# Attention and two gated layers on one core: Strassen's scheme for a whole block in the first layer's second pass, and an order amended by a table

## The chip, the core and the metric

The kernel runs on one core of a Trainium2 chip. The metric is the time of one execution in device microseconds, from the first to the last instruction of the program with what lies around it; smaller is better. Each kernel is run several times and the median is given.

## The reference, cut to what matters

Attention within chunks of 64 positions, then two layers that every token passes. All arrays are float32; there are 4608 tokens (8 x 576) of 512 features.

```
out = softmax(q_chunk @ k_chunk.T / 8) @ v_chunk        # 8 heads of 64, chunks of 64
x   = out as 4608 tokens x 512
g   = x @ w_gate            # 512 x 1536
val = x @ w_val             # 512 x 1536
x   = (silu(g) * val) @ w_out        # 1536 x 512     first layer
h   = x @ w_in              # 512 x 2048
out = (h * sigmoid(1.702 h)) @ w_out2   # 2048 x 512  second layer
```

Because single products of the fast format are too coarse, every float32 operand is split in a high part and a rest ("hi" and "lo"), and each product is made of three: hi by hi, hi by lo, lo by hi (helper `mm3`, lines 406 to 408).

## The kernel before

**Tiles and passes.** The tokens are cut in nine blocks of 512 (`NB`, `BT`). The hidden features of each layer are cut in halves, so there are four passes over the nine blocks: passes 0 and 1 for the first layer, 2 and 3 for the second. Pass 0 also makes the attention of the next blocks and turns weights into hi and lo on the way (`conv_tile`, `conv_part`, lines 476 to 484); pass 0's sums of a block go to DRAM (`y_dram`) and pass 1 loads them and adds its own. In pass 1 the weights of layer 2 are converted.

**First product.** In a pass of layer 1 a block has three groups (`group_products`), each of four hidden tiles of 128 (two of the gate, two of the value). A group's product is made by Strassen's scheme: seven products (`product`) of 12 matmuls of 256 columns in place of eight, written to two banks of PSUM, and put together by ScalarE copies (tile `u`) and VectorE additions (tile `c`, line 399).

**Second product.** `gated` takes silu of the gate on ScalarE, multiplies on VectorE (tile `h`), and splits into `hh` and `hl`. `second` then multiplies with a weight tile `o` (three matmuls of 512 columns into one of four banks, `ys`): per block 6 hidden tiles by 4 output tiles, 24 such steps, without Strassen. `block_sum` adds the four banks to what pass 0 left (`yv`, then `xr`), and `x_to_dram` makes from a finished block the seven combinations of its token quarters (`token_combos`), hi and lo, and stores them for layer 2 (`x_dram`). In layer 2 both products use Strassen's scheme (`group_gated`, `last_product`), and the blocks' inputs are loaded again (`x_load`).

**What sets the order.** Every step is recorded as an operation with an engine, an estimate of its length and a priority (`Program.op`). `order` plans the five queues (TensorE "PE", VectorE "DVE", ScalarE "ACT", GpSimd "POOL", and one DMA queue on SP) from these; `dues` works back from the end; `emit` repeats this 28 times with amended keys, judges each order by `replay` and keeps the best. The instructions are then issued engine by engine in that order, and each engine takes its own strictly in turn. Buffers come from rings: `o` has three tiles of 512 KB, `x` eight, `xr` one.

## Time and profile before

| | |
|---|---|
| median of three runs | 1688.71 us (1688.47 to 1689.58) |
| the profiled execution | 1689.54 us |
| its span, first to last instruction | 1687.2 us |
| TensorE busy | 1658.1 us, 98% |
| VectorE, ScalarE, GpSimd busy | 65%, 53%, 43% |
| share of the chain that ended last that lies on TensorE | 84% |
| mean busy share of the 16 DMA engines, per 1/40 of the span | between 0.3 and 0.9 or more, mostly 0.7 to 0.9 |

How to read it: the numbers of a row are microseconds from the start of the span, unless marked ns. TensorE's matmuls are pipelined, so a row's duration is longer than the step from one matmul's start to the next; the step is read from two starts. Idle time stands with the engine that was waited for. The passes can be told by their DMAs: the last store of pass 0's sums is issued at 543 us, the first load of them in pass 1 at 547 us, and the first weight tile of layer 2's second product at 961 us.

### The profile page before, as it was taken

What the parts mean: (1) busy time and instruction counts of PE and PEld (TensorE: products, weight loads), DVE (VectorE), ACT (ScalarE), POOL (GpSimd) and SP (SyncE); (2) the same over time, 40 slices, a digit from 0 to 9 for tenths busy, and PEclk for the clock granted to TensorE, in tenths of its full rate; (3) what the DMA queues carried; (4) which work ended last, traced back from release to release, by engine and by line L of the source; (5) the groups of instructions that cost most, each with busy time, mean ns of one, the idle gap of its engine ahead of it and who ended that gap; (6) DMA issues with size and microseconds to landing.
All of it is one profiled execution on the core that took longest, in us unless ns stands there. A gap on an engine that the chain in (4) does not pass through costs nothing.

```text
span 1687.2 us, 36353 instructions
## 1 busy us (share of the span) xinstructions
PE 1658.1 (98%) x14428; PEld 1579.5 (94%) x14428; DVE 1098.8 (65%) x1606; ACT 892.2 (53%) x1511; POOL 726.0 (43%) x736
## 2 busy tenths in 40 slices
PE   7989999999999999999999999999999999999998
PEld 7878999889999999999999999999999999999998
DVE  6878877787764566644544477787755556555556
ACT  6876677777644444433333456555544444444443
POOL 2675516564444555541211235676731133333333
PEclk8999999999999999999999999999999999999999
DMA  7567788887899899887679998999989977777773
GB/s 293 177 237 276 271 273 301 284 288 258 281 333 342 305 330 325 304 283 243 233 247 337 375 334 299 312 318 317 311 262 339 348 231 232 233 238 236 235 257 109
DMA packets 184153, 472.65 MB, mean 280 GB/s; under 512 B 19760, under 2 KB 44848, under 8 KB 183728
## 3 DMA queue, kind: packets, MB, share of 16 engines
q1 hardware_dynamic: 183984, 470.34, 81.7%
q8 instruction: 114, 1.87, 0.4%
q14 instruction: 55, 0.45, 0.1%
HBM read 331.84 MB, written 138.41 MB: 279 GB/s over the span
## 4 chain that ended last, share of the span: by engine, by line
PE 84%; DVE 4%; DMA 3%; ACT 3%; issue 2%; POOL 2%; SPq 0%; POOLq 0%; DVEq 0%; ACTq 0%
PE banks L406 28%; PE banks L408 27%; PE banks L407 27%; PE banks L667 1%; DMA od_b<-ws 1%; DVE c L399 1%; PE banks L662 1%; DMA raw<-in_moe_w_out 1%; DVE xt L399 1%; DVE t L481 1%; PE banks L732 1%; ACT L718 0%; POOL ws L399 0%; DMA raw<-in_moe_w_in 0%; POOL wc L399 0%
## 5 line engine op out<-in xcount | busy, mean ns | idle before, releaser
L399 DVE TENSOR_TENSOR c<-u,banks 128x512 f32<-128x512 f32 x312 | 213.2, 683 | 307.4 <-PE banks L408 192.2
L406 PE MATMUL banks<-x,wc 128*128 128x256 f32 x1044 | 297.5, 285 | 3.2 <-ACT u L390 2.9
L407 PE MATMUL banks<-x,wc 128*128 128x256 f32 x1044 | 294.6, 282 | 0.0
L408 PE MATMUL banks<-x,wc 128*128 128x256 f32 x1044 | 294.5, 282 | 0.0
L390 ACT COPY u<-banks 128x512 f32<-128x512 f32 x261 | 152.9, 586 | 248.4 <-PE banks L408 247.2
L406 PE MATMUL banks<-x,wb 128*128 128x256 f32 x744 | 213.3, 287 | 4.2 <-ACT x L390 2.4
L406 PE MATMUL banks<-x,wa 128*128 128x256 f32 x744 | 211.3, 284 | 2.1 <-DVE c L399 1.6
L407 PE MATMUL banks<-x,wb 128*128 128x256 f32 x744 | 211.5, 284 | 0.8 <-DVE x L399 0.8
L408 PE MATMUL banks<-x,wb 128*128 128x256 f32 x744 | 211.4, 284 | 0.0
L407 PE MATMUL banks<-x,wa 128*128 128x256 f32 x744 | 210.0, 282 | 1.1 <-POOL x L399 1.1
L406 PEld LDWEIGHTS banks<-x,wc 128*128 128x128 f32 x1044 | 198.3, 190 | 13.2 <-ACT u L390 6.0
L408 PE MATMUL banks<-x,wa 128*128 128x256 f32 x744 | 210.0, 282 | 0.0
L407 PEld LDWEIGHTS banks<-x,wc 128*128 128x128 f32 x1044 | 198.4, 190 | 6.5
L408 PEld LDWEIGHTS banks<-x,wc 128*128 128x128 f32 x1044 | 198.9, 191 | 0.0
L406 PE MATMUL banks<-hh,o 128*128 128x512 f32 x432 | 173.5, 402 | 0.3 <-ACT hh L390 0.3
L408 PE MATMUL banks<-hh,o 128*128 128x512 f32 x432 | 172.6, 400 | 0.0
L407 PE MATMUL banks<-hl,o 128*128 128x512 f32 x432 | 170.8, 395 | 0.2 <-DVE hl L399 0.2
L974 ACT ACTIVATE xr<-c 128x512 f32<-128x512 f32 x136 | 86.0, 632 | 153.9 <-DVE c L399 149.8
L406 PEld LDWEIGHTS banks<-x,wb 128*128 128x128 f32 x744 | 142.7, 192 | 11.2 <-ACT x L390 2.5
L407 PEld LDWEIGHTS banks<-x,wb 128*128 128x128 f32 x744 | 142.8, 192 | 5.3 <-DVE x L399 1.0
L406 PEld LDWEIGHTS banks<-x,wa 128*128 128x128 f32 x744 | 141.0, 190 | 6.8 <-DVE c L399 2.8
L407 PEld LDWEIGHTS banks<-x,wa 128*128 128x128 f32 x744 | 140.9, 189 | 4.7 <-POOL x L399 1.7
(227 smaller groups left out, 4494.6 us busy)
## 6 DMA issues: line engine op xcount, KB each, us to landing
x<-x_dram SPq DMA_DIRECT2D x182, 512.0 KB, 5.5
o<-od_b SPq DMA_DIRECT2D x119, 512.0 KB, 4.6
o<-od_a SPq DMA_DIRECT2D x102, 512.0 KB, 5.1
x_dram<-x SPq DMA_DIRECT2D x56, 512.0 KB, 5.8
wd_b<-ws SPq DMA_DIRECT2D x56, 256.0 KB, 4.7
od_b<-ws SPq DMA_DIRECT2D x56, 256.0 KB, 4.6
raw<-in_moe_w_out SPq DMA_DIRECT2D x44, 255.8 KB, 4.8
wd_a<-ws SPq DMA_DIRECT2D x42, 256.0 KB, 4.2
```

Of the source, the lines that this page charges most:

```text
L390: op("act", act_us(n), lambda: nc.scalar.copy(out=dst.ap, in_=cut(src.ap)), [src], [dst], prio, near=near)
L399: lambda: e.tensor_tensor(out=dst.ap, in0=of_a(a.ap), in1=of_b(b.ap), op=by), [a, b], [dst], prio, near=near)
L406: nc.tensor.matmul(o, ah, bh, start=first, stop=False, **kind)
L407: nc.tensor.matmul(o, ah, bl, start=False, stop=False, **kind)
L408: nc.tensor.matmul(o, al, bh, start=False, stop=last, **kind)
L481: op("dve", dve_us(n), lambda: nc.vector.scalar_tensor_tensor(out=t.ap.bitcast(I32), in0=t.ap, scalar=-4096 * up, in1=word(1).bitcast(F32) ...
L662: nc.tensor.matmul(un.s.ap[h64(b), a, h64(g)], un.q.ap[h64(a), cs], un.k.ap[h64(a), cs], start=True, stop=True)
L667: nc.tensor.matmul(un.o.ap[h64(b), a, h64(2 * g + c)], un.v.ap[h64(a), cs], un.e.ap[h64(a), cs], start=True, stop=True)
L732: nc.tensor.transpose(pt.ap[:, cs], e.ap[:, cs], ident.ap)
L974: op("act", act_us(512), lambda: nc.scalar.activation(out=h.ap, in_=c.ap, func=AF.Gelu_apprx_sigmoid), [c], [h], prio, "gelu")
```

## The change

Five things are changed together.

1. In pass 1 the second product of a whole block is made by Strassen's scheme. The gated values of the block's six hidden tiles are kept as four quarters (256 tokens by 384 hidden features, `hidden`, `gated_quarters`); `hidden_part` makes seven combinations and their hi and lo (768 elements per partition each); `second_part` multiplies each with its weight combination in three steps of six matmuls of 256 columns, 21 steps in place of 24, into three banks. The result is added to pass 0's sums, which are loaded straight into `xr`. The weight combinations are made in pass 0 (`y_combos`, `out_pair`) and stored in `yw_dram`; a load of `o` brings two of the 21.
2. `x_to_dram` writes the lo over its own source (`xt`, `xr`) and the hi into the area that holds the hidden parts. Only the last block but one is made into `x` tiles, which stay in SBUF and are what layer 2 begins with; pass 2 takes the blocks in the order 7, 0 to 6, 8 and pass 3 begins with block 8, whose tiles are still there (`BLOCKS`).
3. The rings `q`, `k`, `v`, `h`, `e`, `yv`, `hh`, `hl` become places in three areas (`Stage`: `sr`, `sf`, `sp`) that pass 1 uses in another way.
4. `replay` is gone. The planner's order is amended by a table, `PLACES`: it names operations that move to another engine or behind another operation, some hundreds for each engine.
5. Some of the planner's estimates are altered (0.72 for 0.8, 1.18 for 1.3, 6.0 for 8.0).

```
+PLACES = {
+    "pe": (
+        "4:9,44,61,22,19,21,8 5:26,10,18,24,17,27,52 7:13 11:15,6,20 78:54,69 23:28 25:16 209:244 "
...
+    def amended(self, seq):
+        queue = {eng: [o for o in seq if o.eng == eng] for eng in self.FREE}
+        runs = [(eng, *run.split(":")) for eng, places in PLACES.items() for run in places.split()]
+        for eng, _, ns in runs:
+            for n in ns.split(","):
+                o = self.ops[int(n)]
+                queue[o.eng].remove(o)
+                o.eng = eng
+        for eng, behind, ns in runs:
+            i = queue[eng].index(self.ops[int(behind)]) + 1 if int(behind) >= 0 else 0
+            queue[eng][i:i] = [self.ops[int(n)] for n in ns.split(",")]
...
+        j = passes[1][1].index(g)
+        def out_pair(prio):
+            t0, t1 = [conv_tile((g.name, "o", i), g.outs[i], prio) for i in range(2)]
+            for n, (m, src, cut) in enumerate(y_combos(t0, t1, prio)):
...
+                store(yw_dram[:, i], s, [yw_done[i]], prio + n)
...
     def x_to_dram(xb, b, prio):
...
+        if b == NB - 2:
+            X[2, b] = [None] * 7
+            for n, (m, src, cut) in enumerate(combos):
+                i = ORDER[2].index(m)
+                X[2, b][i] = x = ring["x"].new([P, 2, 2, HT], F32R)
+                split(*[x.part(lambda ap, c=c: ap[:, c]) for c in range(2)], src, 512, prio + n, ("dve", "pool")[n % 2], cut)
+                store(x_dram[1][:, b, i], Buf(lambda x=x: x.ap.rearrange("p c a t -> p (c a t)"), None, None, x), [xd[1][b][i]], prio + n + 2)
+            return
...
+                t = stage[2].take(n % 4 * 3, 2)
...
+            lo = Buf(lambda src=src, cut=cut: cut(src.ap).bitcast(F32R), None, None, src)
...
+    YORDER = "1326574"
...
+    def gated_quarters(y, j, c, prio):
+        js = slice(j * 256, (j + 1) * 256)
...
+            op("act", act_us(512), lambda ap=ap, i=i: nc.scalar.activation(
+                out=ap(), in_=c[i].ap[:, :, 0], func=AF.Silu), [c[i]], qs, prio, "silu")
+            op("dve", dve_us(512), lambda ap=ap, i=i: nc.vector.tensor_tensor(
+                out=ap(), in0=ap(), in1=c[i].ap[:, :, 1], op=ALU.mult), [*qs, c[i]], qs, prio)
...
+    def hidden_part(y, label, prio):
...
+            tt(src, b22, b11, ALU.subtract, 768, prio, T_ENG[1])
...
+        hi, lo = [stage[2].take(k % 2 * 6 + 3 * c, 3) for c in range(2)]
+        split(hi, lo, src, 768, prio, Y_LO[k])
+        if label == "1":
+            tt(b11, b12, b11, ALU.subtract, 768, prio, T_ENG[0])
+        elif label == "3":
+            tt(b12, b22, b12, ALU.subtract, 768, prio, T_ENG[2])
+        elif label == "6":
+            tt(src, src, b21, ALU.subtract, 768, prio + 2, T_ENG[3])
...
+        if k % 2 == 0:
+            n = min(2, 21 - k)
+            w4 = ring["o"].new([P, 2, 2, 256], F32R)
...
+        def fn():
+            ts = slice(j * 256, (j + 1) * 256)
+            for e in range(2):
+                es = slice(e * P, (e + 1) * P)
+                mm3(m.ap[:, e], w.ap[:, 0, es], w.ap[:, 1, es], hi.ap[:, ts], lo.ap[:, ts],
+                    e == j == 0 and not goes_on, j == 2, skip_group_check=True)
+        op("pe", OS, fn, [w, hi, lo], [m], prio)
...
+    BLOCKS = [range(NB), range(NB), [NB - 2, *range(NB - 2), NB - 1], [NB - 1, NB - 2, *range(NB - 2)]]
...
-                elif end and nxt[0] < NPASS:
-                    x_load(*nxt, start[nxt[0]][nxt[1]] - 18)
+                elif end and nxt == (3, 0):
+                    X[3, b] = xs
+                elif end and nxt[0] < NPASS and nxt != (2, 0):
+                    x_load(nxt[0], BLOCKS[nxt[0]][nxt[1]], start[nxt[0]][nxt[1]] - 18)
```

What the built programs show at three places follows. First ScalarE in the opening, where pass 0's first block is made and the exponentials of the first units stand among the silu of the first products (`h`, after the change `sr`). The kernel before:

```order
L916 ACT_TABLE_LOAD
L916 ACTIVATE h<-banks 128x256
L478 ACTIVATE wb_273<-wb_273,offset 128x512 x2
L735 COPY c<-banks 128x512
L718 ACT_TABLE_LOAD
L718 ACTIVATE e<-e 128x512
L476 ACTIVATE t<-wa_318,offset 128x512
L390 CAST x<-banks 128x4x128
L390 COPY xr<-banks 128x4x128
L916 ACT_TABLE_LOAD
```

The same place after the change:

```order
L661 ACTIVATE t<-wa_231,offset 128x512
L936 COPY c<-banks 128x512 x2
L919 ACTIVATE sf<-sf 128x512
L1136 ACT_TABLE_LOAD
L1136 ACTIVATE sr<-banks 128x256
L573 CAST x<-banks 128x4x128 x2
L573 COPY xr<-banks 128x4x128
```

The exponential of the next unit now stands ahead of the first silu, so that one load of the table stands there in place of three.

Second VectorE within a block of pass 1. Before, where `c` is a sum of the first product, `h` the gated values, `hl` their lo, `xr` the block's sum:

```order
L399 TENSOR_TENSOR c<-u,banks 128x512
L399 TENSOR_TENSOR xr<-yv,banks 128x512
L399 TENSOR_TENSOR c<-u,banks 128x512
L399 TENSOR_TENSOR h<-h,c 128x512
L399 TENSOR_TENSOR c<-u,banks 128x512
L399 TENSOR_TENSOR hl<-h,hh 128x512
```

After the change, where `sf` and `sr` hold the quarters and `sp` the lo of a combination:

```order
L581 TENSOR_TENSOR c<-u,banks 128x512 x4
L581 TENSOR_TENSOR sp<-sf,sp 128x768
L581 TENSOR_TENSOR sp<-sr,sp 128x768 x2
L581 TENSOR_TENSOR sf<-sf 128x768
L581 TENSOR_TENSOR sr<-sr,sf 128x768
L581 TENSOR_TENSOR sf<-sr,sf 128x768
L581 TENSOR_TENSOR xr<-xr,banks 128x2x256 x2
L581 TENSOR_TENSOR sp<-sr,sp 128x768
L581 TENSOR_TENSOR sp<-sf,sp 128x768
L581 TENSOR_TENSOR sr<-sr 128x768
```

Seven lo and four combinations of 768 elements and nine additions into `xr` per block stand in the place of six lo of 512 and four additions.

Third the DMA queue on SP in pass 1. Before, where `yv` is a part of pass 0's sums and `o` a weight tile of the second product:

```order
L386 DMA x_dram_71<-e 128x512
L383 DMA o<-od_a_83 128x1024
L383 DMA x<-x_dram_70 128x1024 x2
L386 DMA x_dram_71<-q 128x512
```

After the change, at the end of a block's stores:

```order
L569 DMA x_dram_72<-sp 128x512
L569 DMA x_dram_72<-xr 128x2x256
L569 DMA x_dram_72<-xt 128x512 x3
L566 DMA xr<-y_dram 128x2x512 x2
L566 DMA o<-yw_dram 128x1024 x6
L566 DMA x<-x_dram_71 128x1024
```

The load of the next block's sums into the one `xr` now stands behind the stores from that `xr`, and weight tiles for the next block stand behind it.

## Rows read from the trace of the kernel before

**Rows 1.** The page's first part: busy time, share of the span, instructions.
```profile
PE 1658.1 (98%) x14428; PEld 1579.5 (94%) x14428; DVE 1098.8 (65%) x1606; ACT 892.2 (53%) x1511; POOL 726.0 (43%) x736
```

**Rows 2.** Busy time of each engine by stretch of the span, clock and DMA.
```profile
core 0: us, PE busy (x) PEld busy (x) DVE busy (x) ACT busy (x) POOL busy (x), PEclk, DMA share, GB/s
0.00:103.00 103.00, 87.89 (x1024) 78.01 (x1024) 77.46 (x114) 79.37 (x128) 53.91 (x45) 0.95 0.65 227
103.00:543.00 440.00, 434.94 (x4547) 399.68 (x4546) 327.54 (x509) 288.77 (x476) 217.15 (x241) 1.00 0.83 290
543.00:963.00 420.00, 419.62 (x2898) 390.26 (x2898) 227.07 (x321) 164.78 (x289) 154.09 (x163) 1.00 0.85 298
963.00:1003.00 40.00, 39.25 (x326) 38.65 (x324) 29.43 (x40) 22.27 (x40) 14.57 (x11) 1.00 0.96 334
1003.00:1687.20 684.20, 676.43 (x5640) 672.93 (x5640) 437.33 (x625) 336.95 (x581) 286.24 (x279) 1.00 0.81 268
```

**Rows 3.** TensorE's instructions in order of time in pass 1: start, duration.
```profile
950.15 0.39 PE L406 MATMUL banks<-hh,o 128*128 128x512 f32 x1
...
950.86 0.28 PE L406 MATMUL banks<-x,wa 128*128 128x256 f32 x1
...
952.29 0.39 PE L406 MATMUL banks<-hh,o 128*128 128x512 f32 x1
```

**Rows 4.** Who TensorE waited for, 0 to 103 us: total, times, longest.
```profile
PE banks L732 <- DVE c L723: 4.0, 2, 3.6
PE banks L406 <- ACT x L390: 2.4, 1, 2.4
```

**Rows 5.** ScalarE in order of time in the opening: start, duration.
```profile
30.13 1.28 ACT L916 ACT_TABLE_LOAD   x1
31.43 0.38 ACT L916 ACTIVATE h<-banks 128x256 f32<-128x256 f32 x1
...
33.60 1.28 ACT L718 ACT_TABLE_LOAD   x1
```

**Rows 6.** The chain that ended last, 23 to 28 us: start, length.
```profile
23.79 0.21 PE banks L408
```

**Rows 7.** GpSimd's instructions by form, 38 to 100 us: busy, mean ns, idle.
```profile
L399 POOL TENSOR_TENSOR o<-t,o 128x512 fp32r<-128x512 f32 x6 | 8.9, 1484 | 7.0 <-ACT o L390 6.9
```

**Rows 8.** VectorE's instructions by form: 500 to 750 us, 750 to 950, whole span.
```profile
L399 DVE TENSOR_TENSOR c<-u,banks 128x512 f32<-128x512 f32 x64 | 43.7, 682 | 58.0 <-ACT u L390 43.6 <-PE banks L408 14.1
L399 DVE TENSOR_TENSOR h<-h,c 128x512 f32<-128x512 f32 x32 | 28.5, 891 | 9.0 <-ACT h L934 8.6
L481 DVE SCALAR_TENSOR_TENSOR t<-t,raw 128x256 int32<-128x256 f32 x22 | 16.7, 765 | 9.3 <-ACT raw L478 8.9 <-issue 0.4
...
L399 DVE TENSOR_TENSOR h<-h,c 128x512 f32<-128x512 f32 x26 | 18.6, 715 | 9.8 <-ACT h L934 9.3
...
L399 DVE TENSOR_TENSOR h<-h,banks 128x256 f32<-128x256 f32 x12 | 4.8, 412 | 0.4 <-ACT h L916 0.4
```

**Rows 9.** Busy time by stretch, two blocks of pass 1; columns as in rows 2.
```profile
823.00:870.00 47.00, 47.00 (x328) 43.79 (x327) 22.34 (x34) 16.30 (x29) 9.45 (x7) 1.00 0.72 247
...
917.00:963.00 46.00, 46.00 (x318) 42.49 (x317) 22.23 (x30) 19.21 (x32) 11.67 (x9) 1.00 1.00 372
```

**Rows 10.** DMA issues, median us to landing: two at 823 to 870, one at 917 to 963.
```profile
yv<-y_dram SPq DMA_DIRECT2D x4, 256.0 KB, 3.4
x_dram<-q SPq DMA_DIRECT2D x4, 256.0 KB, 5.1
...
x_dram<-k SPq DMA_DIRECT2D x4, 256.0 KB, 7.2
```

**Rows 11.** Loads of weight tile `o` in pass 2, 1100 to 1150 us, and that stretch.
```profile
L383 SPq DMA_DIRECT2D o<-od_b x7: 319/320/390, 1109.3 to 1126.7; - x7
...
DMA to landing us min/median/max: 3.6/4.8/5.5
...
1100.00:1150.00 50.00, 50.00 (x420) 49.82 (x419) 41.51 (x58) 30.67 (x55) 34.19 (x41) 1.00 0.91 308
```

More of the change, by code (lines that the diff above doesn't have):

```diff
@@ L67, in new, with __init__, turn, take @@
         return b
+class Stage:
+    UNIT = 256
+    def __init__(self, pool, name, tags):
+        self.ring, first = Ring(pool, name, 1), 0
+        self.places = {}
+        for tag, n in tags:
+            self.places[tag] = Place(self, [first + 2 * i for i in range(n)])
+            first += 2 * n
+        self.size = first
+    def turn(self, dtype):
+        self.now, self.last = self.ring.new([P, self.size * self.UNIT], dtype), [None] * self.size
+    def take(self, first, n):
+        b = self.now.part(lambda ap: ap[:, first * self.UNIT:(first + n) * self.UNIT])
+        last = list(dict.fromkeys(a for a in self.last[first:first + n] if a is not None))
+        b.prev = b.prev + last
+        self.last[first:first + n] = [b] * n
+        for a in last:
+            a.next.append(b)
+        return b
+class Place:
+    def __init__(self, stage, homes):
+        self.stage, self.homes, self.count = stage, homes, 0
+    def new(self, shape, dtype=F32):
+        b = self.stage.take(self.homes[self.count % len(self.homes)], 2)
+        self.count += 1
+        if len(shape) == 3:
+            flat = b.make
+            b.make = lambda: flat().rearrange("p (a b) -> p a b", a=shape[1])
+        return b
 class Banks:
-    HOME = {"ya": (0, 2), "yb": (2, 2), "ga": (4, 1), "gb": (5, 1), "gab": (4, 2), "s": (6, 1), "a": (7, 1), "sa": (6, 2)}
+    HOME = {"ya": (0, 2), "yb": (2, 2), "ga": (4, 1), "gb": (5, 1), "gab": (4, 2), "y0": (0, 1), "y1": (1, 1), "y2": (2, 1), "s": (6, 1), "a": (7, 1), "sa": (6, 2)}
     def __init__(self, tile):
@@ new lines, in amended @@
+    def amended(self, seq):
[9 more added lines that the diff above has]
+            queue[eng][i:i] = [self.ops[int(n)] for n in ns.split(",")]
+        rank = {o: i for i, o in enumerate(seq)}
+        for todo in queue.values():
+            last = len(seq)
+            for o in reversed(todo):
+                last = rank[o] = min(rank[o], last)
+            todo.reverse()
+        made = set()
+        while len(made) < len(seq):
+            heads = [todo[-1] for todo in queue.values() if todo and made.issuperset(todo[-1].deps) and made.issuperset(todo[-1].follows)]
+            o = min(heads, key=lambda o: (rank[o], o.n))
+            queue[o.eng].pop()
+            made.add(o)
+            yield o
@@ L1120, in block_sum @@
         s = ring["yv"].new([P, BT])
-        if p == 0:
-            copy(s, ys[e], 512, prio, "act" if e % 2 else "dve")
-            yd[b, e] = Buf(None)
-            store(dram, s, [yd[b, e]], prio)
-            return
-        load(s, dram, prio - 14, [yd[b, e]])
-        if e == 0:
-            xr[b] = ring["xr"].new([P, KD, BT])
-        tt(xr[b].part(lambda ap: ap[:, e]), s, ys[e], ALU.add, 512, prio)
-        if e == KD - 1:
+        copy(s, ys[e], 512, prio, "act" if e % 2 else "dve")
@@ new lines, in block_sum, with hidden, ap @@
+        yd[b, e] = Buf(None)
+        store(dram, s, [yd[b, e]], prio)
+    YORDER = "1326574"
+    class Hidden:
+        pass
+    def hidden():
+        y = Hidden()
+        y.homes = [[stage[1].take(3 * n, 3) for n in range(2)], [stage[0].take(3 * n, 3) for n in range(2)]]
+        return y
+    def gated_quarters(y, j, c, prio):
+        js = slice(j * 256, (j + 1) * 256)
+        for i in (1, 0):
+            qs = [q.part(lambda ap: ap[:, js]) for q in y.homes[i]]
+            whole = stage[1 - i].now
+            def ap(whole=whole):
+                return whole.ap[:, :1536].rearrange("p (n c) -> p n c", n=2)[:, :, js]
+            op("act", act_us(512), lambda ap=ap, i=i: nc.scalar.activation(
+                out=ap(), in_=c[i].ap[:, :, 0], func=AF.Silu), [c[i]], qs, prio, "silu")
+            op("dve", dve_us(512), lambda ap=ap, i=i: nc.vector.tensor_tensor(
+                out=ap(), in0=ap(), in1=c[i].ap[:, :, 1], op=ALU.mult), [*qs, c[i]], qs, prio)
@@ L1173, in attention_two_moe_kernel @@
         attend(u, -40 + 4 * u, -60+3*u, bufs, ("sa", "gab", "yb", "ya")[u])
+    stage[2].turn(F32R)
     OW = {}
```

254 lines of the change are left out of this document (144 added, 110 removed), and 161 rows, old and new, of the table PLACES.

## The prediction

> **What bounds the kernel now.** I read the page's busy times first, then the stretches, then what TensorE waited for in each. TensorE is busy for 98% of the span [rows 1], and the stretches say where the other 2% lie [rows 2]. In pass 1 (543 to 963 us) it is idle for 0.4 us of 420, over the turn to layer 2 for 0.8 of 40, and in layer 2 for 7.8 of 684, nearly all of it after the last matmul. The waits are in pass 0: 15.1 us of the first 103 and 5.1 of the next 440. So work taken from TensorE in pass 1 is time won one for one, provided that the engines and queues that feed it keep up, and what a new order can win lies in pass 0 alone.
>
> **The change part by part.**
>
> *Second product of pass 1.* Twelve matmuls of 256 columns take 1.43 us, from 950.86 to 952.29 [rows 3]; six take 0.715. The first product's 21 x 1.43 = 30.0 us of a block stay. A block of pass 1 lasts 420 / 9 = 46.67 us [rows 2], which leaves 16.65 for the 24 old steps, 0.69 each (one alone, from 950.15 to 950.86, reads 0.71 [rows 3]). The 21 new steps take 15.0. That is 1.65 us for each of nine blocks, -15 us (-18 by the single step); a block falls to 45.0. The short matmuls load weights twice as often for their columns; in layer 2, where every matmul is of that form, TensorE still idles for next to nothing [rows 2, 11], so I add nothing.
>
> *What VectorE takes on in pass 1.* The trace has no operation of 768 elements. The nearest are one of 256 (412 ns) and one of 512 (682 ns) [rows 8]; the step of 270 ns for 256 elements gives 0.95 us. Of a block before: 12 sums `c`, 6 gates, 6 lo, 4 additions and 4 combinations, in the trace 22.3 us where no weights are converted [rows 9]. After: 12 sums x 0.68, 6 gates x 0.72, 11 operations x 0.95, 9 additions x 0.68, 4 combinations and 3 or 4 lo x 0.7: 8.2 + 4.3 + 10.5 + 6.1 + 5.4 = 34.5 us of 45, 77%. In the first four blocks the conversion for layer 2 adds four pairs of operations at about 1.35 (0.77 and a little less [rows 8]): 40 us, 89%. Does TensorE then wait? Two rows bound it. Pass 2 ran at 83% VectorE from 1100 to 1150 us and TensorE did not idle at all [rows 11]; 103 to 543 us had 74% and 5.1 us of idle time, 0.6 per block [rows 2]. Nine blocks then cost between 0 and 5 us, and below nothing is excluded since pass 1 has only 0.4 us to give back. I take 2, nearer the first row, whose steps are the same Strassen steps; for the range I let it go to 10 because 89% is above both rows. What is queued behind a late lo on VectorE are the sums `c` that free TensorE's banks, so a delay there reaches the first product too.
>
> *DMA in pass 1.* Weight tiles of a block rise from 6 x 512 KB to 21 x 256 KB, 3.1 to 5.5 MB. The undisturbed block moved 247 GB/s, 11.6 MB in 47 us [rows 9]; it becomes 14 MB in 45 us, 310 GB/s. Conversion and the next pass's weights add to that: pass 1's mean is 298, 51 above the undisturbed block [rows 2, 9], so that 360 is to be expected over stretches. The trace has 372 GB/s over 46 us with TensorE never idle [rows 9], and bursts of `o` loads 2.9 us apart (1109.3 to 1126.7, seven) on the same three buffers, landing in 4.8 [rows 11]. A burst in pass 1 will need a tile of two steps with some product between each 2.7 us. I add nothing for it, and price the case that it fails among the rivals.
>
> *New waits on SP.* The load of the next block's sums waits until the last store from `xr` has landed, and six weight tiles stand behind it. From the end of a block: store of a hi 5.1 [rows 10], a lo at 1.5 where GpSimd makes it [rows 7], its store 5.1, two or three copies and issues of about 2, the tile behind it 4.8 [rows 11]: 19 us, 22 with the load of the sums (3.4 [rows 10]) ahead of it. By the order TensorE has 16 products and 6 steps to do until it needs that tile, 16 x 1.43 + 6 x 0.715 = 27 us. Hidden by 5 us; no cost.
>
> *Turn to layer 2.* Before, seven tiles came by DMA and TensorE idled 0.8 us [rows 2]. Now the tiles of block 7 are made by copies and lo's after its last addition, while block 8's last sums stand between them on VectorE: an addition, two combinations, three sums, one combination and the lo, eight operations of 0.7, 5.5 us, against four products, three of them block 8's and one of the new pass, 4 x 1.43 = 5.7, less 1 for the copy and hand-overs. So about 1 us more; 0 to 4 for the range. Seven loads go, here and at the start of pass 3, where nothing waited for them: nothing. The loads of x behind them on SP come earlier; nothing waits for these either.
>
> *Opening and pass 0.* The new order moves most here and the trace of before prices little of it. Two table loads of 1.28 us, as at 30.13 and 33.60 us, leave ScalarE in the opening, when TensorE was waiting for its copies [rows 4, 5]: -2.6. The Trainium skill (ScalarE: Activation LUTs, What ACT_TABLE_LOAD costs) adds a drain of 1.38 us to each switch, 2.66 in all, so that it would be -5.3 and the time 1670; the trace disagrees, the next activation starting 0.02 us after the load [rows 5]. Some 27 additions for weights move from GpSimd at 1.48 [rows 7] to VectorE at 0.68 or a little more. That shortens GpSimd's chain between 70 and 100 us, for which TensorE waits little, and fills VectorE, at 77 us of the first 103 [rows 2], by 18 us to over 90%. The two longest waits of the opening, 4.0 and 2.4 us [rows 4], hang on VectorE and ScalarE. Bounds: all 15 + 5 us of idle time gone, and with it the stretch at half speed, would be -22 or so and can't be had: the first products run at 23 us, after waits for the first tokens, with 0.21 us per matmul [rows 6], the lower of TensorE's two levels (1.2 GHz; the granted clock is 0.95 over the first 103 us [rows 2]), and the loads and the chain ahead of them stay; the other end is +6, an opening in which VectorE is the bound. I take -4, nearest to the priced table loads, with -12 to +6 kept.
>
> *End.* The last sums move from GpSimd to VectorE, which saves under a microsecond of the 7 after the last matmul: 0.
>
> Sum: -15 + 2 + 1 - 4 = -16 from the profiled execution's 1689.5: 1673.5. That execution is 0.8 us above the median of the runs shown, so **1673**.
>
> **The rivals.**
>
> *The order wins more.* If the opening and pass 0 lose 14 us of their 20 and not 4, the time is 1663. For it: nearly all idle time lies there, and the built order differs there on every engine. Against: of the waits of the first 103 us the two longest [rows 4] hang on one chain of the first tokens.
>
> *The order loses.* If the moves to VectorE make it the bound of the opening, +5 in place of -4: 1682. Near it lies the case in which the table does nothing and Strassen's scheme alone counts (1677).
>
> *VectorE is held off by GpSimd (slower).* A gate took 715 ns where GpSimd was nearly idle and 891 where it converted weights [rows 8]. If each of the 11 new operations and 4 combinations waited for half a GpSimd instruction, 0.74 us [rows 7], the converting blocks would need 40 + 11 = 51 us of VectorE for 45 of TensorE: +6 in four blocks and 1 in the others, 29 us in place of the 2 of the sum, 1700. It decides from the point where the mean of the 768s passes 1.3 us. Against it: the row's increase is 0.18, and many conversions move off GpSimd. The Trainium skill (SBUF, "SBUF — State Buffer", SBUF: two separate sides) states the strict form: VectorE with two operands in SBUF and GpSimd lock the shared ports for a whole instruction, and the loser blocks. By that rule this rival is what comes; the gates' 0.18 [rows 8] says that it bites in part only.
>
> *The turn-around on SP is late (slower).* At 372 GB/s a store took 7.2 us to land, not 5.1 [rows 10]. Two stores, a load and a tile at 2 us more each make 30 us against 27: 3 us in each of eight blocks, 24 us, 1697. It decides from landings of about 6.3 us. Against: pass 1 stays under the 372.
>
> **How the numbers follow.** Forecast 0.50 (1666 to 1681), order wins 0.20, order loses 0.13, VectorE held off 0.10, SP late 0.07. A measurement of this kernel can tell 0.2%, 3.4 us, so faster means under 1685.3 and slower over 1692.1. Faster: 0.50 + 0.20 + 0.11 = 0.81; same: 0.02 of the third and 0.05 of the slow ones where they come weakly, 0.07; slower 0.12. The range reaches from 1656 to 1689, the second case's -12 and the first's +10 with the third, and leaves out the tail of the second case and the two last.
>
> **What will show it.** Pass 1 from first to last product at 405 to 408 us, not 420; operations of 768 on VectorE near 0.95 us; VectorE 75 to 90% busy there; `o` loads landing in about 5 us; TensorE's waits in pass 1 at a few microseconds and at the turn 1 to 3; the first 103 us a few shorter. Wrong would be: waits on `sp` or `xr` in each block, DMA at its full share with landings over 7 us, or an opening that takes longer than before.

## The result and the profile after

The changed kernel takes **1660.9 us** (median of four runs, 1656.5 to 1666.5) against 1688.6 for the kernel before in the same series: a ratio of 0.984 with a 95% interval of 0.981 to 0.987. The forecast was 1673 with a range of 1656 to 1689; its likeliest case was to end between 1666 and 1681. So the sign and the range held, and the time lies 12 us under the forecast, next to the rival "the order wins more" (1663).

The first profiled execution happens to be the longest of its four. The traces below are therefore of a second series of the same kernel (median 1659.8), whose profiled span is 1659.8 us. The page of that execution answers to [rows 1]:

```profile
span 1659.8 us, 37397 instructions
PE 1635.6 (99%) x14914; PEld 1586.3 (96%) x14914; DVE 1220.3 (74%) x1895; ACT 891.7 (54%) x1514; POOL 524.7 (32%) x567
```

TensorE's busy time fell by 22 us, GpSimd's by 201, and VectorE's rose by 121. To see where the span went I cut it at TensorE's own milestones, which both kernels have. A block of layer 1 has 21 first products of 12 matmuls, 252 in all, and a pass 2268; the cuts are the starts of the 253rd of them (block 1 begins), the 2269th (pass 1), the 4537th (pass 2), and the 252nd after that (on weight tiles `wa`, `wb`, `wc`). The stretches by these cuts, first of the kernel before, then of the changed one (start and end, length, busy time of each engine with its number of instructions, granted clock, DMA share, GB/s):

```profile
core 0: us, PE busy (x) PEld busy (x) DVE busy (x) ACT busy (x) POOL busy (x), PEclk, DMA share, GB/s
0.00:82.50 82.50, 70.36 (x867) 63.82 (x867) 61.82 (x96) 65.77 (x107) 33.48 (x31) 0.94 0.65 233
82.50:517.90 435.40, 427.36 (x4531) 390.35 (x4528) 330.97 (x507) 291.41 (x477) 226.01 (x239) 1.00 0.82 283
517.90:940.10 422.20, 421.82 (x2918) 392.65 (x2917) 230.35 (x326) 165.06 (x292) 161.20 (x174) 1.00 0.85 294
940.10:978.60 38.50, 38.50 (x289) 36.72 (x288) 20.61 (x30) 18.79 (x31) 10.18 (x8) 1.00 1.01 382
978.60:1687.20 708.60, 700.08 (x5834) 695.98 (x5832) 455.07 (x648) 351.12 (x606) 295.08 (x286) 1.00 0.82 270
```

```profile
0.00:72.70 72.70, 63.58 (x860) 58.08 (x860) 63.45 (x112) 61.52 (x104) 15.66 (x19) 1.00 0.70 253
72.70:499.60 426.90, 424.18 (x4534) 389.19 (x4527) 336.90 (x549) 286.48 (x473) 199.36 (x225) 1.00 0.85 295
499.60:906.20 406.60, 402.81 (x3320) 399.00 (x3320) 306.10 (x450) 172.91 (x290) 102.55 (x115) 1.00 0.96 340
906.20:953.20 47.00, 45.99 (x381) 45.20 (x380) 38.81 (x53) 23.98 (x39) 8.72 (x5) 1.00 0.99 366
953.20:1659.80 706.60, 699.09 (x5834) 694.86 (x5832) 475.00 (x733) 346.82 (x609) 198.39 (x204) 1.00 0.79 268
```

The opening is 9.8 us shorter, the rest of pass 0 8.5, pass 1 and the turn together 7.1 (460.7 to 453.6), the rest 2.0. Sum: 27.4 us, the whole difference of the two spans. So the larger part of the gain lies ahead of pass 1, where the forecast had put 4 us, and pass 1, where it had put 12, gave 7.

Idle time of a busy column is a rough measure, since a matmul reads 0.28 us where the next starts 0.12 behind it [rows 3]. I therefore also added up, per stretch, what TensorE's steps from start to start take beyond the usual step of their size (0.119 us for 256 columns, 0.2325 for 512), where that is over 0.025. These waits, from before to after: opening 28.2 to 19.7, pass 0 39.6 to 31.5, pass 1 0.7 to 6.6, turn 0.1 to 2.1, rest 6.5 to 6.7. What is left without the waits fell from 459.9 to 444.8 us over pass 1 and the turn: **15.1 us** of columns. A step of the new second product can be read directly, six matmuls from 552.74 to 553.45 and the next six from there to 554.16, 0.71 us each:

```profile
552.74 0.28 PE L589 MATMUL banks<-sp,o 128*128 128x256 f32 x1
...
553.45 0.28 PE L589 MATMUL banks<-sp,o 128*128 128x256 f32 x1
...
554.16 0.28 PE L589 MATMUL banks<-sp,o 128*128 128x256 f32 x1
```

What TensorE waited for in the opening (0 to 100 us), in answer to [rows 4] (waiting group, releaser: total, times, longest), and in pass 1 (530 to 930 us):

```profile
PE banks L589 <- ACT xr L573: 2.0, 1, 2.0
PE banks L1452 <- POOL ident masks.py:199: 1.4, 1, 1.4
PE banks L933 <- DVE sf L917: 1.2, 1, 1.2
PE banks L933 <- DVE sf L924: 1.1, 1, 1.1
PE banks L933 <- DVE c L924: 1.1, 1, 1.1
PE banks L590 <- DVE x L581: 1.0, 1, 1.0
...
PE banks L589 <- DMA o<-yw_dram: 3.3, 6, 1.5
PE banks L589 <- ACT u L573: 0.7, 1, 0.7
PE banks L589 <- DVE xr L581: 0.4, 1, 0.4
```

The first chain of tokens, which cost 4.0 us on VectorE's `c` and 2.4 on ScalarE's `x`, now has single waits of 2 us and less. In pass 1 most of the named waits of this trace are for the second product's weight tiles. In the trace of the first series pass 1 is as long (406.5 us, 6.6 of them waits), and there VectorE is named for more than those tiles are (530 to 925 us):

```profile
PE banks L590 <- DVE sp L581: 1.2, 3, 0.8
PE banks L589 <- DMA o<-yw_dram: 0.9, 2, 0.7
PE banks L589 <- DVE xr L581: 0.8, 1, 0.8
PE banks L589 <- ACT u L573: 0.7, 1, 0.7
```

### The profile page after: what moved, and what is told of

Read it like the earlier page. It is cut to its first block, busy times and chain, and to the rows that moved or that the text cites. A ratio compares the mean times of both kernels' runs of the same rounds, so it can differ in the third digit from the quotient of the medians.

```text
span 1664.6 us, 37397 instructions
## 1 busy us (share of the span) xinstructions
PE 1639.1 (98%) x14914; PEld 1588.4 (95%) x14914; DVE 1218.1 (73%) x1895; ACT 891.6 (54%) x1514; POOL 527.3 (32%) x567
## 4 chain that ended last, share of the span: by engine, by line
PE 82%; DMA 8%; DVE 5%; ACT 2%; issue 2%; POOL 1%; SPq 0%; POOLq 0%; DVEq 0%; ACTq 0%
PE banks L589 27%; PE banks L591 26%; PE banks L590 26%; DMA x_dram<-sp 2%; DMA o<-yw_dram 1%; PE banks L868 1%; PE banks L863 1%; DMA wd_b<-ws 1%; PE banks L933 1%; DMA x_dram<-xr 1%; DMA od_b<-ws 1%; ACT sp L573 1%; DMA o<-od_b 1%; DMA xr<-x_dram 1%; DMA xr<-y_dram 1%
## 5 line engine op out<-in xcount | busy, mean ns | idle before, releaser
L589 PE MATMUL banks<-sp,o 128*128 128x256 f32 (+1 forms) x594 | 195.1, 328 | 2.2 <-DMA o<-yw_dram 1.1
L590 PE MATMUL banks<-sp,o 128*128 128x256 f32 (+1 forms) x594 | 192.0, 323 | 1.2 <-DVE sp L581 1.2
L591 PE MATMUL banks<-sp,o 128*128 128x256 f32 (+1 forms) x594 | 192.0, 323 | 0.0
L589 PEld LDWEIGHTS banks<-x,wb 128*128 128x128 f32 x744 | 142.1, 191 | 8.5 <-DVE c L581 2.4
L590 PEld LDWEIGHTS banks<-x,wb 128*128 128x128 f32 x744 | 142.2, 191 | 2.3 <-DVE x L581 1.0
L589 PEld LDWEIGHTS banks<-x,wa 128*128 128x128 f32 x744 | 141.1, 190 | 2.8 <-DVE c L581 1.0
L591 PEld LDWEIGHTS banks<-x,wb 128*128 128x128 f32 x744 | 142.2, 191 | 0.0
```

What stands on the lines that cost most here:

```text
L589: nc.tensor.matmul(o, ah, bh, start=first, stop=False, **kind)
L590: nc.tensor.matmul(o, ah, bl, start=False, stop=False, **kind)
L591: nc.tensor.matmul(o, al, bh, start=False, stop=last, **kind)
```

## The experiments

Lengths of the five stretches, each cut at the same milestones, from the windows of each trace; medians are of several runs each, the stretches of one execution, which need not lie at the median. Kernels with the same matmuls differ in a stretch by waits and by the granted clock; a microsecond or two between two traces is scatter.

| kernel | median us | opening | pass 0 | pass 1 | turn | rest |
|---|---|---|---|---|---|---|
| before | 1688.6 to 1689.9 | 82.5 | 435.4 | 422.2 | 38.5 | 708.6 |
| before, planner's order alone | 1709.3 | 90.0 | 441.7 | 421.5 | 38.4 | 715.5 |
| before, 42 additions on VectorE | 1684.6 | 80.4 | 434.5 | 421.6 | 40.2 | 709.6 |
| changed | 1660.9; 1659.8 | 72.7 | 426.9 | 406.6 | 47.0 | 706.6 |
| changed, empty table | 1697.0 | 87.2 | 433.0 | 410.5 | 50.3 | 714.1 |
| changed, table up to pass 1 | 1675.5 | 73.5 | 425.9 | 409.6 | 50.3 | 712.0 |
| changed, table's places, 217 additions back on GpSimd | 1693.9 | 81.4 | 436.4 | 406.4 | 50.9 | 716.2 |
| changed, table's engines, planner's places | 1685.5 | 80.6 | 434.3 | 406.1 | 49.8 | 712.7 |
| changed, half the weight tiles of pass 1 | 1655.6 | 73.8 | 427.5 | 400.6 | 46.4 | 708.0 |
| changed, a third of the low parts | 1662.8 | 72.6 | 427.0 | 410.0 | 46.8 | 707.4 |
| changed, low parts twice | 1690.5 | 73.6 | 425.8 | 431.6 | 49.1 | 708.9 |
| changed, weight loads of pass 1 in halves | 1658.8 | 71.9 | 425.8 | 402.7 | 46.8 | 706.3 |
| changed, these and layer 2's in halves | 1659.6 | 73.3 | 427.6 | 405.2 | 46.3 | 707.0 |

### The same kernel again

> The changed kernel once more, unaltered. Its four executions lay between 1656.5 and 1666.5 us, those of the kernel before between 1687.9 and 1689.6. If the scatter of 10 us is a property of the kernel (a feed with little slack, DMA or VectorE in pass 1), these runs spread over 6 to 12 us again, median 1658 to 1664, and their traces differ in TensorE's waits while its columns cost the same. If it belonged to that one chip or moment, they lie within 3 us of each other.

Measured: 1659.8 us (1659.6 to 1661.6, five runs), ratio 0.983 (0.981 to 0.984). The spread is 2 us here and 10 in the first series. The two traces have the same columns to 0.3 us; the longer one (span 1664.6) has 5.0 us more waits: 0.7 in the opening, 1.9 in pass 0 and 2.3 behind the turn, none more in pass 1. By the second expected answer the scatter belonged to that series and not to the program; but kernels below with the same order spread over 6 to 7 us again, so it comes and goes. It is made of single waits in several places. A part of it can be seen (20 to 30 us, first the longer execution, then the second series):

```profile
20.00:30.00 10.00, 9.21 (x133) 8.57 (x134) 8.72 (x18) 8.86 (x15) 2.59 (x2) 0.67 1.03 384
```

```profile
20.00:30.00 10.00, 7.89 (x142) 7.09 (x143) 9.40 (x20) 9.86 (x17) 2.59 (x2) 1.00 1.03 405
```

The granted clock there was 0.67 in the one and 1.00 in the other, at the same place of the same program.

### The table, and what it makes up for

The changed kernel with an empty table:

```
-PLACES = {
-    "pe": (
...
+PLACES = {}
```

> The changed kernel with an empty table: the planner's own order, all else kept. Theory A (the forecast's split: 15 us from TensorE's columns, 4 from the opening and pass 0, of which the table has a part): 1662 to 1672. Theory B (the trace's split: the first 550 us lost 14 us of waits, and the table did it, and it also holds the waits of pass 1 down): 1675 to 1690, with at least 14 us more of waits ahead of pass 1. Theory C (the table does nothing): 1656 to 1666.

The table up to pass 1, the planner's order from there on:

```
+        planned = {o: o.eng for o in self.ops}
+        made = list(self.amended(seq))
+        cut = next(i for i, o in enumerate(made) if o.eng == "pe" and o.prio < 9999 and o.n >= 2271)
+        head = set(made[:cut])
+        tail = [o for o in seq if o not in head]
...
+        for o in made[:cut] + tail:
             o.fn()
```

> The table's order up to TensorE's first product of pass 1, the planner's own order (and engines) from there on. Theory B: it keeps the whole of what the opening and pass 0 won, so it lies under the kernel without the table by 10 to 16 us, and above the full table by whatever the table is worth in passes 1 to 3 (2 to 10 us): 1663 to 1675. If the table's worth lies in pass 1 and behind it, it is within 4 us of the kernel without the table.

The kernel before without its replay:

```
-        for i in range(2 * self.ROUNDS):
...
-            last = sum(self.replay(seq, j) for j in range(3)) / 3
-            if best is None or last < best[0]:
-                best = last, seq
...
-        for o in best[1]:
+            seq = self.order()
+        for o in seq:
             o.fn()
```

> The kernel before with its choice among 28 replayed orders taken out: twelve rounds of the planner with keys blended by a quarter, the last order taken, as the changed kernel makes it before its table. If the planner's order is as good as the replayed one, 1686 to 1692, and the empty-table kernel shows what Strassen's scheme and the tokens kept in SBUF are worth by themselves (13 to 18 us). If the replay was worth something, 1693 to 1705, and part of the table's worth only makes up for it.

Measured, all on one chip with before at 1689.6: empty table 1697.0 (ratio 1.005, 1.004 to 1.007), table up to pass 1 1675.5 (0.993, 0.991 to 0.994), the kernel before without its replay 1709.3 (1.012, 1.011 to 1.013). Taking out the replay costs **19.7 us**; what the changed kernel adds to that order without a table (Strassen's scheme in pass 1, tokens that stay in SBUF, areas, estimates) gives back **12.3**; the table gives **37.2**, of which 21.5 come from its part up to pass 1 and 15.7 from the rest. 19.7 - 12.3 - 37.2 = -29.8, the way from 1689.6 to 1659.8. Without its table the changed kernel is slower than the kernel before. This is theory B of the expectations, but each of the three times lies beyond the range that I gave for it; the other theories are out.

The 12.3 are not what Strassen's scheme gives in pass 1. By the table of stretches, pass 1 and the turn take 459.9 us in the kernel before without its replay and 460.8 in the changed kernel with an empty table: the 15 us of columns that the scheme saves all come back there as waits. The gain lies in pass 0 (8.7), the opening (2.8) and the rest (1.4), and which of the other alterations brings it was not tested. Only with the table do pass 1 and the turn fall to 453.6.

### Engines or places

The table does two things: it gives 217 operations of GpSimd to VectorE (and 43 the other way), and it moves operations within their queues. The places kept, the 217 back on GpSimd:

```
+        planned = {o: o.eng for o in self.ops}
+        made = list(self.amended(seq))
+        for o in made:
+            if planned[o] == "pool":
+                o.eng = "pool"
+        for o in made:
             o.fn()
```

> The changed kernel in the table's order, but with the 217 operations that the table moves from GpSimd to VectorE left on GpSimd, at the place in its queue that the order gives them. Theory A: the places are what the table wins by, the engine hardly matters since VectorE is no bound and GpSimd has room: 1658 to 1668. Theory B: GpSimd at 1.48 us for an addition of 512 elements, against 0.68 on VectorE, is what TensorE waited for in the opening and pass 0: 1675 to 1700, with 8 us more of waits in the opening, 5 more in pass 0 and some in every pass behind.

The engines kept, given to the planner before it plans, and no places:

```
+        for eng, places in PLACES.items():
+            for run in places.split():
+                for n in run.split(":")[1].split(","):
+                    o = self.ops[int(n)]
+                    if o.eng != eng:
...
+                        o.eng = eng
...
-        for o in self.amended(seq):
+        for o in seq:
             o.fn()
```

> The changed kernel with the table's 260 changes of engine (217 from GpSimd to VectorE, 43 the other way) given to the planner before it plans, and none of the table's places: the order is the planner's own for these engines. With neither the kernel took 1697.0 us, with the places alone 1693.9, with both 1659.8. Theory A, the change of engine is what pays: 1660 to 1672. Theory B, engines and places pay only together (VectorE, at 18 to 20 us of every 20 in the opening, must take each addition at its moment): 1680 to 1697.

Measured: places alone 1693.9 us (ratio 1.002, 1.001 to 1.004), engines alone 1685.5 (0.998, 0.997 to 0.999). Against the empty table's 1697.0 that is -3.1 and -11.5; both together are -37.2. (In the first of the two the 43 operations that the table moves the other way still run on GpSimd, so it isn't the places alone to the last operation.) **Some 23 of the 37 us exist only if both are there.** The first of the two expectations for each run (the engine hardly matters; the engine is what pays) fails, and the time of each lies in the range of theory B.

The table of stretches tells where the two need each other, and it isn't the opening. There they nearly add up: places 5.8 us, engines 6.6, both 14.5. In pass 0 each alone costs time, 3.4 and 1.3 us, and both together win 6.1; over the turn and the rest the places cost 2.7, the engines win 1.9, and both win 10.8. What ties them together there no run takes apart. What each alone leaves undone in the opening can be seen from 40 to 60 us, at the same time but not at the same work, first of the changed kernel, then with the 217 on GpSimd, then with the engines alone:

```profile
40.00:60.00 20.00, 19.90 (x224) 17.89 (x222) 19.93 (x32) 18.08 (x32) 7.65 (x5) 1.00 0.59 198
```

```profile
40.00:60.00 20.00, 16.84 (x155) 14.81 (x154) 14.87 (x21) 13.77 (x23) 13.87 (x10) 0.83 0.38 128
```

```profile
40.00:60.00 20.00, 19.77 (x187) 18.39 (x187) 16.72 (x27) 17.26 (x29) 6.57 (x4) 0.92 0.46 154
```

What TensorE waited for in the first 110 us, of the two kernels with one factor each in that order:

```profile
PE banks L595 <- POOL x L586: 4.5, 1, 4.5
PE banks L938 <- DVE sf L929: 3.5, 3, 1.6
PE banks L595 <- POOL sp L586: 3.2, 1, 3.2
```

```profile
PE banks L598 <- DVE x L590: 6.0, 1, 6.0
```

With both, VectorE is busy for 19.93 of 20 us and TensorE for 19.90. With the 217 on GpSimd TensorE is busy for 16.84: it waits 3.2 us there, until 46.8, for a low part from GpSimd (the 4.5 us end at 109.5, in pass 0). With the planner's places it is busy for 19.77 in this window; it had waited 6.0 us in one piece, until 22.2, for a low part of the first tokens that VectorE makes.

The same question put to the kernel before: the additions and low parts of the opening's weights on VectorE, planner and replay kept:

```
-            split(*[w.part(lambda ap, c=c: ap[:, :, c]) for c in range(2)], src, 512, prio, "pool")
+            split(*[w.part(lambda ap, c=c: ap[:, :, c]) for c in range(2)], src, 512, prio, "dve")
...
-        tt(s3, t0, t1, ALU.subtract, 512, prio, "pool", a[0], a[0])
+        tt(s3, t0, t1, ALU.subtract, 512, prio, "dve", a[0], a[0])
```

> The kernel before with one alteration: the additions and low parts that make the opening's weights (42 operations, mostly 512 elements) run on VectorE instead of GpSimd; planner and replay as they were. If GpSimd's 1.48 us was what the opening waited for whatever the order, the opening's waits (28.2 us with the 21 products of each of block 0's groups counted) fall by 5 to 9 us: 1680 to 1684. If it takes an order made for it, VectorE becomes the bound: 1686 to 1695.

Measured: 1684.6 us, ratio 0.998 (0.997 to 0.999), a gain of 4 us; the opening falls from 82.5 to 80.4. It is between the two expectations: the engine alone is worth something here too. Where the 4 us lie isn't shown, since the profiled execution is the longest of its ten (1688.1 us).

### What the waits in pass 1 are

Pass 1 and the turn hold 8.7 us of waits where there were 0.8. Three edits take the two suspects apart. Half the weight tiles:

```
-                y.w[k + m] = w4.part(lambda ap, m=m: ap[:, m])
+                y.w[k + m] = w4.part(lambda ap: ap[:, 0])
...
-                 yw_dram[:, k:k + n].rearrange("p a b c -> p (a b c)"), prio - 14, yw_done[k:k + n])
+                out=rd(w4.ap[:, :1].rearrange("p a b c -> p (a b c)")), in_=yw_dram[:, k:k + 1].rearrange("p a b c -> p (a b c)")),
```

> The changed kernel, but each load of combined output weights in pass 1 brings one of its two combinations, and both steps multiply with that one (this leaves out half of those weights): 2.6 MB less in each block of about 15. Theory A, the added 8 us of waits in pass 1 and at the turn are the DMA's (that stretch ran at a share of 0.96 and 339 GB/s): waits on those tiles go, pass 1 keeps 1 to 3 of its 6.6 us of waits, 1653 to 1657. Theory B, they are VectorE's or the order's: within 2 us of 1660, the weights landing earlier for nothing.

A third of the low parts of the hidden combinations, and the same low parts made twice:

```
-        split(hi, lo, src, 768, prio, Y_LO[k])
+        copy(hi, src, 768, prio)
+        w = 768 if y.first else 256
...
+            out=lo.ap[:, :w], in0=src.ap[:, :w], in1=rd(hi.ap)[:, :w], op=ALU.subtract), [src, hi], [lo], prio)
```

> The changed kernel, but from the second block on the low parts of the hidden combinations in pass 1 are made for a third of their 768 elements only (the rest keeps old values): seven operations per block of 0.42 in place of 0.97 us, some 30 us less of VectorE's 304 in the 395 us of pass 1. Theory A, the waits in pass 1 are the DMA's: within 2 us of 1660. Theory B, they are VectorE's (sums that free TensorE's banks late behind the long operations): 1653 to 1657, pass 1's waits at 1 to 3 us in place of 6.6.

```
+            for i in range(2):
+                {"dve": nc.vector, "pool": nc.gpsimd}[o.eng].tensor_tensor(
+                    out=lo.ap, in0=src.ap, in1=rd(hi.ap), op=ALU.subtract)
```

> The changed kernel, but the low parts of the hidden combinations in pass 1 are made twice over (the second time the same values): seven operations of 0.97 more in each of nine blocks, 61 us, VectorE from 77% to about 92% of pass 1, above 100% in the blocks that also convert weights. The forecast's view (VectorE has room of its own, only its share of the time counts): 1666 to 1676, about 2 us for each converting block and little in the others. If TensorE hangs on each of these operations (the chain from gate to low part to product has no slack): 6 us for each block, 1700 to 1715. If VectorE's queue absorbs it: under 1664.

Measured: 1655.6 (ratio 0.980, 0.978 to 0.982), 1662.8 (0.984, 0.982 to 0.986) and 1690.5 (1.002, 1.001 to 1.003). Pass 1 of the three in that order:

```profile
501.30:901.90 400.60, 400.29 (x3320) 398.23 (x3319) 308.31 (x450) 172.65 (x290) 102.27 (x115) 1.00 0.86 293
```

```profile
499.60:909.60 410.00, 403.32 (x3319) 399.04 (x3318) 280.25 (x450) 172.63 (x290) 96.15 (x115) 1.00 0.95 337
```

```profile
499.40:931.00 431.60, 409.82 (x3320) 401.64 (x3319) 361.43 (x505) 172.93 (x290) 107.99 (x116) 1.00 0.92 320
```

And the largest waits of the third in it (530 to 955 us):

```profile
PE banks L590 <- DVE sp L1393: 11.3, 16, 1.5
PE banks L589 <- DVE xr L581: 4.2, 4, 1.6
PE banks L589 <- DVE c L581: 2.7, 4, 1.6
```

With half the tiles' bytes pass 1 falls from 406.6 to 400.6 us, its waits from 6.6 to 0.7, while VectorE does the same 308 us of work. With 26 us less of work on VectorE nothing is won (1662.8 is a microsecond above the range of theory A and five above that of theory B); pass 1 even reads 3.4 us longer in that one trace, again with the weight tiles as the largest wait (5.4 us in eight). **The added waits of pass 1 go with the bytes of these tiles**, also where the trace of the first series names VectorE. The third run shows where VectorE's room ends: 55 us more of it (361 of 432) cost pass 1 25.0 us, the largest part in 16 waits for a low part, 0.7 us each. The 1690.5 us lie between the forecast's view and "no slack on each": about 0.5 us for each of the 63 operations added.

Which of the tiles come late can be read from their issues. Of the six named waits of the changed kernel the longest, 1.5 of the 3.3 us, is for a tile that SP issued at 600.79 us, right behind the two loads of `xr`, and that landed 8.5 us later. The other five are for tiles that landed 5.9 to 7.3 us after their issue, and four of these were issued as soon as TensorE had freed the buffer.

The landing of these tiles was 5.6 us for 512 KB in the changed kernel and 3.5 for 256 KB in the half one (issues in the program, KB each, median us to landing):

```profile
o<-yw_dram SPq DMA_DIRECT2D x90, 512.0 KB, 5.6
```

```profile
o<-yw_dram SPq DMA_DIRECT2D x99, 256.0 KB, 3.5
```

This suggested a version with all bytes, but in loads of half the size:

```
+                for m in range(n):
+                    nc.sync.dma_start(out=rd(w4.ap[:, m].rearrange("p b c -> p (b c)")), in_=yw_dram[:, k + m].rearrange("p b c -> p (b c)"))
```

> The changed kernel, but each 512 KB load of two combined output weights in pass 1 is issued as two loads of 256 KB at the same place in the queue. With half the bytes left out the waits of pass 1 fell from 6.6 to 0.7 us and a load landed in 3.5 us, not 5.6. If TensorE waits for the landing of a tile's first half only, it now comes earlier: pass 1's waits 2 to 4 us, 1656 to 1658. If the queue's total bytes set it, the halves land no earlier: 1659 to 1662, and 95 more issues on SP may cost up to 2 us.

and the same for layer 2's tiles (`d[:, n, m]` in place of `d[:, n]`):

> The changed kernel with the weight loads of the second product issued in halves of 256 KB in pass 1 (as in the run before) and in layer 2 as well. If TensorE waits for a tile's first half where it waits for these loads at all, pass 1 keeps 2 to 4 of its 6.6 us of waits and the one wait of about 1 us at the turn to layer 2 shrinks: 1655 to 1658, with the interval of its ratio under that of the changed kernel (0.9814). If the gain of the run before was scatter, 1659 to 1662; if 216 more issues on SP hold up the queue in layer 2, 1662 to 1668.

Measured: 1658.8 us (1655.3 to 1660.9; ratio 0.982, 0.980 to 0.984) and 1659.6 (1657.5 to 1663.3; 0.983, 0.981 to 0.984). Both intervals overlap the changed kernel's (0.981 to 0.984), so these versions are not shown to be better. The mechanism does show: halves land in 4.8 to 5.0 us, and the wait for them in pass 1 (525 to 930 us) is down from 3.3 us to

```profile
PE banks L589 <- ACT u L573: 0.7, 1, 0.7
PE banks L589 <- DMA o<-yw_dram: 0.4, 1, 0.4
```

in the first of the two and absent in the second, where waits for VectorE and ScalarE of 3 us in sum stand in its place. In the first one's trace, the shortest execution of its four, pass 1 is 3.9 us shorter (402.7); in the second's it is 1.4 shorter, and there TensorE meets again at the other engines most of what it gains at the tiles.

## Why the prediction was right, and where it was wrong

**Second product, -15: right.** 15.1 us of columns went over pass 1 and the turn, and the step is 0.71. But the check that I had set myself, 405 to 408 us from first to last product of pass 1 (it reads 406.6), came true by errors that cancel: 21.6 us of columns left pass 1, 6.5 of them only moved into the turn, where second-product steps now stand behind pass 2's first products, and 5.9 us of waits came in.

**VectorE in pass 1, +2: right in the load, and not the cause.** Operations of 768 elements take 0.99 us on average, 0.95 forecast. In blocks without conversion VectorE is busy for 34.2 to 36.0 us of 45 (771 to 861 us), 34.5 forecast; in those with it for 34.7 to 37.8 (545 to 726 us), 40 forecast, which was 2 to 5 us too much:

```profile
L581 DVE TENSOR_TENSOR sp<-sr,sp 128x768 fp32r<-128x768 f32 x31 | 29.6, 961 | 11.9 <-ACT sp L573 11.9
L581 DVE TENSOR_TENSOR sp<-sf,sp 128x768 fp32r<-128x768 f32 x24 | 23.7, 986 | 17.3 <-ACT sp L573 13.5 <-DMA x_dram<-sp 3.7
L581 DVE TENSOR_TENSOR sf<-sf 128x768 f32<-128x768 f32 x8 | 7.6, 955 | 0.1
```

Less load won nothing, so this term was about 0 at this load.

**DMA in pass 1, 0: wrong, +6.** The bytes were forecast well enough (310 GB/s undisturbed and about 360 in stretches; 340 on average, at a share of 0.96). The step that failed is the conclusion that a stretch of 372 GB/s without idle time in the old kernel [rows 9] proves such traffic harmless. There, tiles were used in another rhythm. Here a burst of 10 or 11 tiles passes three buffers, and the tiles land after 5.6 us, against the 4.8 I had used [rows 11]. That the bytes bring the waits is shown by the run with half of them; that the rhythm and the three buffers turn bytes into waits is my reading, with no run of its own.

**SP's new waits, 0, and the turn, +1: the first right but for one block, the second small by one.** For sums that stand on `xr` TensorE waits 0.4 us (0.8 in the first series), but one tile behind the `xr` loads cost 1.5 us; the turn has 2.1 us of waits.

**Opening and pass 0, -4: wrong, -18.** This is the term that carries the error. I priced it by the two table loads that I could see leave (8 loads now stand between 28 and 96 us, there were 10) and set all idle time of 20 us, with the stretch at half speed 22, as a bound that couldn't be had. That idle time is only a part of the waits: by the steps there were 67.8 us of them ahead of pass 1, of which 16.6 went. Three things were missed. First, the replay. I listed its removal among the parts of the change and never priced it; alone it costs 19.7 us, so my neighbour case "the table does nothing and Strassen's scheme alone counts (1677)" is off by 20: it is 1697.0, slower than before. Secondly, the table. It is worth 37 us, 21.5 ahead of pass 1, and it needs its engines and places together. Thirdly, I took VectorE at over 90% as the danger of the opening (the rival at 1682). It is at 19.9 of 20 us from 40 to 60 us, and TensorE is busy for 19.90 of them; with the same engines but the planner's places the opening takes 80.6 us in place of 72.7. A full second engine is not yet the bound.

**The stretch at half speed** was in my bound as something that stays. In the changed kernel's second trace it is gone: before, 24 steps of about 0.21 us, as in [rows 6], stand between 23.4 and 29.4 us and 13 more between 38.4 and 41.4, at a granted clock of 0.66 (20 to 30 us) and 0.91 (30 to 50); after, the clock reads 1.00. 37 steps by 0.09 us are 3.3 us. In the first profiled execution that stretch was there (18 steps, 0.67) and its opening was 0.8 us longer, so it is not won for certain. The row of before:

```profile
20.00:30.00 10.00, 8.11 (x97) 7.52 (x98) 8.33 (x13) 6.94 (x13) 3.10 (x3) 0.66 0.84 334
```

**Layer 2 and the end, 0: -2.** The table's part behind pass 1 is not idle: without it the rest takes 712.0 us in place of 706.6. (0.9 of the 2 us lie behind the start of the last matmul, 7.4 us before and 6.5 after.) It made up there for the planner's plain order, which I had not priced either.

**The rivals.** "The order wins more" described what happened, at a chance of 0.20; its 14 us of waits less ahead of pass 1 measured 16.6. VectorE held off by GpSimd did not come: it was to decide from a mean of 1.3 us for the 768s, which is 0.99. But the prediction's ground for that, that the lock bites in part only, is not what the trace shows: an operation that is caught waits in full, and only 9 of 93 are caught (last section). SP late did not come as priced, 3 us in each of eight blocks: it was to decide from landings of about 6.3 us, and the tiles' median is 5.6 (3.2 to 9.5). In one block it came in part, with the 1.5 us above.

So that the net was in the range is in part luck: -14 in one term and +6 in another partly cancelled, and the range had been drawn out far. Its lower end, 1656, doesn't even follow from the terms, whose lowest values (-18, 0, 0 and -12) add up to 1659. With the terms as measured: -15.1 (columns) - 18.3 (opening and pass 0) + 7.9 (waits in pass 1 and at the turn) - 2.0 (rest) = -27.5.

What stays open: why the same program has a spread of 10 us in one series and 2 in another, and what grants the clock at 20 us in one execution and not in the next.

## What to carry to other kernels

Price what a change takes away in the planning as well as in the work: a removed search over orders cost 20 us here, more than the 15 us of columns that the headline edit saves, and without the table those 15 us were eaten by waits where they were saved. Moving work to a faster engine and moving it to its right place can be worth little each and much together, so test them as two factors with all four corners. And a trace without waits at some DMA rate does not vouch for another burst at the same rate; price a new burst by its own landing time, buffers and steps.

## What the runs showed of the hardware

An operation of 768 elements on VectorE takes 0.954 us on average (70 of 93, the longest 0.960) when no GpSimd instruction overlaps it, and 1.087 (23 of 93, the longest 2.02) when one does. Which of the 23 lose time depends on who began first. Nine began while a GpSimd instruction had 0.20 to 1.21 us left; each ended 0.81 to 0.82 us after that instruction, and so took 1.01 to 2.02. Five found less than 0.09 us left, and nine began first or together with GpSimd; these 14 took 0.946 to 0.961. The other way round, six casts of GpSimd began 0 to 0.42 us after a VectorE operation of 768, and all ended 1.20 to 1.22 us after its start. A row of each kind follows (start, duration): at 755.52 GpSimd is first and VectorE is held; at 672.80 VectorE is first, and a cast that took 0.40 us at 755.04 takes 0.78.

```profile
755.04 0.40 POOL L575 CAST ws<-st 128x256 fp32r<-128x256 f32 x1 [6.36 <-DMA od_b<-ws]
755.52 0.74 POOL L581 TENSOR_TENSOR ws<-st,ws 128x256 fp32r<-128x256 f32 x1
755.72 1.36 DVE L581 TENSOR_TENSOR sp<-sf,sp 128x768 fp32r<-128x768 f32 x1 [0.18 <-ACT sp L573]
...
672.80 0.95 DVE L581 TENSOR_TENSOR sp<-sr,sp 128x768 fp32r<-128x768 f32 x1
673.22 0.78 POOL L575 CAST ws<-t 128x256 fp32r<-128x256 f32 x1 [5.16 <-DMA wd_b<-ws]
```

So the two engines do hold each other off, as the Trainium skill (SBUF — State Buffer, SBUF: two separate sides) states of the ports that they share: the one that begins first keeps them for its whole instruction. The mean is low because few operations are caught, not because a caught one loses little; in all the 23 lose 3.1 us. With the low parts made twice 39 of 154 overlap, at 1.21 on average and up to 2.60.

Two executions of one program had a granted clock of 0.67 (a mean over TensorE's two levels) and 1.00 over the same ten microseconds, 20 to 30 us, with TensorE busy 6.4 and 7.2 us in the ten before.
